# Gate/up pairs between the QKV blocks, h in two halves, and a last tile in halves, in a fused local-attention and GLU kernel

## The chip, the core and the metric

The kernel runs on one core of a Trainium2 chip. The metric is the device time of one execution in microseconds (us). A core has TensorE (PE, matmuls into PSUM), VectorE (DVE), ScalarE (ACT), GpSimd (POOL) and SyncE (SP). Each works through its own queue in order, and they wait for each other on semaphores. PEld is PE's loading of weights, which overlaps its matmuls. Transfers (DMA) are issued from the queues of SP, ACT and POOL.

## What is computed

The input x is 2048 rows of 512 values, bfloat16. Cut to what matters:

```
xn  = layernorm(x)                                  # per row
q, k, v = xn @ wqkv                                 # 32 heads of 16
logits[s, w] = q[s] . k[s - 2 w] / 4,  w = 0..7     # masked where s - 2 w < 0
o   = softmax(logits) @ v[s - 2 w];   s = o @ wo
y   = (gelu(xn @ w_gate) * (xn @ w_up)) @ w_down    # 512 -> 1792 -> 512
out = x + s * silu(y)
```

## The kernel before, in words

The rows are cut into four blocks of 512 (j = 0 to 3), each of four tiles of 128 rows. In a block:

- `layer_norm`: DVE takes the statistics of a tile (L303, L304), ACT a square root (L310) and DVE a reciprocal (L316) for blocks 0 and 1; for blocks 2 and 3 POOL does both (`rstd_pool`, L325, L328). DVE normalises (L335), PE transposes (L351), ACT or DVE copies the result into `xnT` (L359, L361).
- `qkv`: twelve groups of four matmuls of 512 columns (block 0: 96 matmuls of 256 columns, in two halves of rows), L430, each into a PSUM tile of the ring `psf` ("f", four tiles). ACT evacuates them: q (L443), k (L449), v (L454, `vst`, four buffers). v goes to DRAM (SP, L403) and comes back shifted for the eight window places as `v_arr` (POOL, four transfers per half block, L496, three buffers).
- `scores`: DVE multiplies q by four shifted k at once (L517, 128 x 2048) and adds pairs of products (L527). Per half of the window there are four products and two adds; PE sums what is left with 8 matmuls into L (L534), ACT takes exp (L546). PE sums over the window (L588), DVE inverts (L598), PE spreads the result (L606), ACT copies it (L616).
- `values`: DVE normalises (L626), multiplies by v (L639) and adds pairs (L649), PE sums into O (L656), ACT evacuates (L667).
- `ffn_pair`: for each of 14 column groups four matmuls for g and four for u (L710), ACT's gelu of g (L720), DVE's product with u, read from PSUM, into h (L727). h shares its buffer with `wqkv_sb`.
- `out_tile`: s from o and wo (L752), y from h and w_down (L764), silu (L775), gate (L778), residual (L785), store (L789). The last tile's s, gate, residual and store are cut at column 384; both parts of s lie in one PSUM tile.

The order of the instructions on each engine is fixed when the kernel is built. The class `Order` (L45) is a list scheduler. Every task has an engine, an assumed duration (the constants of L26 to L38), the tasks that it needs, a priority, and the buffers that it takes and frees; `run` always takes the task that can start first by these assumptions. HOP (L38) is the assumed delay from one engine to another. A chain of `add_main` tasks keeps the QKV, gate/up and output matmuls in program order on PE; transposes, L, sums and O are slotted in where the scheduler expects them to be ready. ACT also issues the loads of the weights (`load_weights`, L842 to L856). All HW transfers share eight semaphores in turn, so an issue can wait for the transfer eight places earlier.

Of the kernel before, what the change touches and what calls it, by code (L numbers as in the profile page):

```python
# [9 lines left out]
ALU = mybir.AluOpType  # L10
# [14 lines left out]

MM = 0.216  # L26
COL16 = 1.1
COL8 = 0.65
TR = 0.28
PROD = 1.14  # L30
HMUL = 0.6
STATS = 0.8
NORM = 0.36
TRCOPY = 0.36
ACT1 = 0.62
ACT2 = 1.06
TABLE = 1.28
HOP = 0.2  # L38
# [6 lines left out]
class Order:  # L45
# [45 lines left out]
    def run(self):  # L91
        left = list(self.tasks)
        while left:
# [10 lines left out]
            if t.eng == "dve" and t.prio >= 1.0:  # L104
                soon = [
                    (self.ready(u), u.seq, u) for u in left
                    if u.eng == "dve" and u.prio <= -1.5 and self.ready(u) is not None
                ]
                if soon and min(soon)[0] < s + 0.4:
                    s, _, t = min(soon)  # L110
# [20 lines left out]
def kernel(  # L131
# [23 lines left out]
    def pool(name, bufs, **kw):  # L155
# [8 lines left out]
    vapool = pool("vapool", 3)  # L164
    prpool = pool("prpool", 6)
# [6 lines left out]
    psf = pool("psf", 4, space=bass.MemoryType.PSUM)  # L172
    psa = pool("psa", 2, space=bass.MemoryType.PSUM)
# [5 lines left out]
        {"xn": 4, "q": 3, "vst": 4, "va": 3, "pr": 6, "attn": 2, "o": 2, "h": 1, "gl": 3, "sg": 3,  # L179
         "f": 4, "a": 2, "O": 1}  # L180
# [5 lines left out]
    wqkv_sb = hpool.tile([P, 3, NC * D + 64], BF16, name="wqkv_sb", tag="h")  # L186
    order.taken["h"].append("wqkv")
# [3 lines left out]
    wd_sb = wpool.tile([P, NF, D], BF16, name="wd_sb")  # L191
    wqkv_v = A_wqkv.rearrange("(k p) n -> p k n", p=P)

    for t in range(TPB):
        eng = nc.sync if t % 2 == 0 else nc.scalar
        eng.dma_start(out=x_sb[:, t, :], in_=x2d[t * P : (t + 1) * P, :])  # L196
# [12 lines left out]
    load_wqkv(0)  # L209
# [6 lines left out]
    x_there = [3.2, 3.5, 3.8, 4.1] + [9.5] * 2 + [12.0] * 2 + [13.5] * 4 + [16.0] * 4  # L216
# [12 lines left out]
    mhalf = cpool.tile([P, TPB], F32, name="mhalf")  # L229
    nc.gpsimd.memset(mhalf[:], -0.5)  # L230
# [63 lines left out]
    rstd_done = {}  # L294

    def layer_norm(j):
# [24 lines left out]
        def rstd_pool(t0, n, deps):  # L321

            def fn():
                r = rstd[:, t0 : t0 + n, 0]
                nc.gpsimd.tensor_scalar(  # L325
                    out=r, in0=mv[:, t0 : t0 + n, 1], scalar1=EPS, scalar2=None, op0=ALU.add
                )
                nc.gpsimd.tensor_tensor(out=r, in0=r, in1=mhalf[:, 0:n], op=ALU.pow)  # L328

            return add("pool", 1.4, fn, deps=deps, prio=prio)  # L330

# [14 lines left out]
        def transpose(t, dep, on_act):  # L346
            def fn():
                tiles["tr", t] = psa.tile([P, NC * P], BF16, name="tr_ps", tag="a")
                for c in range(NC):
                    cs = slice(c * P, (c + 1) * P)  # L350
                    nc.tensor.transpose(tiles["tr", t][:, cs], tiles["xn", t][:, cs], ident[:])  # L351
                if t < 2:
                    warm_up(2 + t, TQ // 2)
# [9 lines left out]
            a = add("pe", TR, fn, deps=[dep], prio=-1.0, takes=[("a", ("tr", t))], frees=[("xn", t)])  # L363
# [13 lines left out]
        elif j == 1:  # L377
            for half in range(2):
                pair = list(ts)[2 * half : 2 * half + 2]
                r = rstd_act(pair[0], 2, [stat(t) for t in pair])  # L380
                for t in pair:
                    transpose(t, norm(t, r), on_act=False)
        else:
            r = rstd_done[j] = rstd_pool(ts[0], TPB, [stat(t) for t in ts])
            for t in ts:
                transpose(t, norm(t, r), on_act=False)
# [10 lines left out]
    v_stored = {}  # L397

# [11 lines left out]
    def qkv(j):  # L410
# [4 lines left out]
        for lo in range(0, TQ, n):  # L415
            for which in range(3):
                for c in range(0, NC, w):
# [57 lines left out]
                    else:  # L475
                        st = add("sp", 0.6, store_v(j, c, lo, n, w), deps=[e], prio=-1.0)

                        v_stored[j] = add(
                            ("dma", key), 3.0, lambda: None, deps=[(st, 0.0)], frees=[("vst", key)]
# [5 lines left out]
    def load_values(j, half):  # L485
        def fn():
            v_arr = vapool.tile([P, DH // 2, VL], BF16, name="v_arr")
            tiles["va", j, half] = v_arr
            SP = PAD + S
            for w4 in range(4):  # L490
# [5 lines left out]
                nc.gpsimd.dma_start(out=v_arr[32 * w4 : 32 * (w4 + 1), :, :], in_=src)  # L496

        issue = add("pool", 2.4, fn, deps=[v_stored[j]], prio=-2.0, takes=[("va", (j, half))])
        v_ready[j, half] = add(("dma", "va", j, half), 7.5, lambda: None, deps=[(issue, 0.0)])
# [5 lines left out]
    def scores(j, prio):  # L505
        exps = []
        for w2 in range(2):
# [21 lines left out]
            def reduce(w2=w2, prods=prods):  # L529
                L = psa.tile([P, TQ], F32, name="L_ps", tag="a")  # L530
                tiles["L", j, w2] = L
                for i in range(2):
                    for w4 in range(4):
# [5 lines left out]
                            stop=(i == 1),  # L539
# [14 lines left out]
            for c in range(NC):  # L554
# [9 lines left out]
                if c % 2 == 1:  # L564
# [3 lines left out]
                            opens=key, closes=key if last else None, frees=[("pr", (*key, c))],  # L568
                        )
                    )  # L570
            r = add(
                "pe", COL8, reduce, deps=[ps[-1]], prio=-0.5, takes=[("a", ("L", j, w2))],
                frees=[("pr", (*key, c)) for c in (0, 2)],
# [44 lines left out]
        s = add("pe", 0.4, sums, deps=[(e, 0.3) for e in exps], prio=-0.4, takes=[("a", ("sum", j))])  # L618
        r = add("dve", 1.15, recip, deps=[s], prio=-1.5, frees=[("a", ("sum", j))])
        b = add("pe", 0.3, spread_back, deps=[r], prio=-0.4, takes=[("a", ("b", j))])  # L620
        b_ready[j] = add("act", ACT1, b_copy, deps=[b], prio=-0.6, frees=[("a", ("b", j))])

    def values(j, prio):
# [10 lines left out]
        for half in range(2):  # L634
# [39 lines left out]
            for i in range(4):  # L674
# [19 lines left out]
                "pe", COL8, reduce, deps=[ps[-1]], prio=-0.5, takes=[("O", (j, half))],  # L694
# [10 lines left out]
    def ffn_pair(j, fc):  # L705
# [17 lines left out]

        def mult():
            if fc == 0:
                tiles["h", j] = hpool.tile([P, NF, TQ], BF16, name="hT", tag="h")
            nc.vector.tensor_tensor(  # L727
                out=tiles["h", j][:, fc, :], in0=tiles["gl", j, fc][:], in1=tiles["u_ps", j, fc][:],
                op=ALU.mult,
            )  # L730
# [7 lines left out]
        h_ready[j, fc] = add(  # L738
            "dve", HMUL, mult, deps=[a, u], prio=-2.0, takes=[("h", j)] if fc == 0 else [],
            frees=[("f", ("u", j, fc)), ("gl", (j, fc))],  # L740
        )


    def out_tile(j, tt, split):
        t = j * TPB + tt
        last = tt == TPB - 1

        def s_mms(cs):
            if cs.start == 0:
                tiles["s", t] = psf.tile([P, D], F32, name="s_ps", tag="f")  # L750
            for c in range(NC):
                nc.tensor.matmul(  # L752
                    tiles["s", t][:, cs],
# [6 lines left out]
        def y_mms(lo, hi):  # L760
            if lo == 0:
                tiles["y", t] = psf.tile([P, D], F32, name="y_ps", tag="f")
            for fc in range(lo, hi):
                nc.tensor.matmul(  # L764
                    tiles["y", t][:],
                    lhsT=tiles["h", j][:, fc, tt * P : (tt + 1) * P],
                    rhs=wd_sb[:, fc, :],
# [4 lines left out]
        def silu():  # L772
            tiles["sil", t] = fpool.tile([P, D], BF16, name="sil")
            tiles["sg", t] = fpool.tile([P, D], BF16, name="sg")
            nc.scalar.activation(out=tiles["sil", t][:], in_=tiles["y", t][:], func=AF.Silu)  # L775

        def gate(cs):
            nc.vector.tensor_tensor(  # L778
                out=tiles["sg", t][:, cs], in0=tiles["sil", t][:, cs], in1=tiles["s", t][:, cs],
# [11 lines left out]
        edges = (0, D) if not split else (0, D - P, D)  # L791
        columns = [slice(a, b) for a, b in zip(edges, edges[1:])]
        y = None
        s = []

        def add_y():
            y = None
            for lo, hi in ((0, NF // 2), (NF // 2, NF)):
                y = add_main(
# [59 lines left out]
    for j in range(NJ):  # L859
        layer_norm(j)  # L860
# [46 lines left out]
```

The softmax here doesn't subtract the row's maximum and nothing guards it: scores larger than these inputs give would overflow.

## Time and profile before

| | us |
|---|---|
| median of 14 runs (lowest to highest) | 231.48 (230.47 to 232.1) |
| the profiled execution, and its span | 231.22, 229.5 |
| PE busy (share) | 222.0 (97%) |
| DVE busy (share) | 193.3 (84%) |
| ACT busy (share) | 111.1 (48%) |
| POOL busy (share) | 28.1 (12%) |
| TensorE clock granted, mean | 0.997 |
| one 128x512 matmul, from one start to the next | 0.216 |
| one product of 128x2048 on DVE, busy; from one start to the next | 1.22; 1.14 |

In the profile a row of a group reads: line, engine, operation, tiles (out<-in), shapes, count | busy time in all, mean ns of one | idle time just before, and what ended it. The chain of work that ended last is followed back from the last instruction: a piece is its start, its length and what it was; matmuls lie end to end there, while their rows overlap by about 0.16 us. The slices cut the span into 40 parts of 5.7 us; a digit is the busy share in tenths. A timeline line is start, length, engine, line and operation, with the idle time before it and what ended that in square brackets. ACTq and SPq are the queues that issue transfers.

### The profile page before, as it was taken

How to read it: one execution, taken by the hardware profiler on the slowest of the kernel's cores; microseconds unless marked ns; L12 is line 12 of the kernel's file. 1: busy time of each engine (PE TensorE's matmuls, PEld its weight loads, DVE VectorE, ACT ScalarE, POOL GpSimd, SP SyncE). 2: the span in 40 equal slices, each digit the busy share in tenths (PEclk: the TensorE clock that was granted, in tenths of full speed). 3: DMA queues.
4: the chain of work that ended last, by engine and by line, in shares of the span. 5: the costliest groups of instructions: out<-in, count | busy, mean ns of one | idle time of the engine just before them, and what ended most of it. 6: DMA issues, size and time to landing. Idle time of an engine off the chain costs nothing.

```text
span 229.5 us, 3272 instructions
## 1 busy us (share of the span) xinstructions
PE 222.0 (97%) x1234; PEld 105.0 (46%) x1234; DVE 193.3 (84%) x270; ACT 111.1 (48%) x167; POOL 28.1 (12%) x67
## 2 busy tenths in 40 slices
PE   7899999899999999999999999999999999999992
PEld 2897554354444434444444444444444444444441
DVE  4899999999999999999999999999759997343222
ACT  3566568477634365454435474434463164334211
POOL 7102930300412000040400002100000000000000
PEclk9999999999999999999999999999999999999998
DMA  5995799599828000054530010900000100000010
GB/s 153 350 381 175 158 205 362 167 281 339 206 38 186 3 0 23 23 123 111 119 68 3 0 46 23 211 0 0 1 3 23 46 23 1 3 0 0 23 45 25
DMA packets 15072, 22.64 MB, mean 99 GB/s; under 512 B 1472, under 2 KB 11984, under 8 KB 15056
## 3 DMA queue, kind: packets, MB, share of 16 engines
q0 software_dynamic: 2592, 8.54, 16.9%
q1 hardware_dynamic: 8592, 7.57, 10.5%
q10 hardware_dynamic: 3872, 6.32, 7.9%
q8 instruction: 9, 0.15, 0.3%
q14 instruction: 7, 0.06, 0.1%
HBM read 18.22 MB, written 4.21 MB: 98 GB/s over the span
## 4 chain that ended last, share of the span: by engine, by line
PE 94%; DMA 3%; DVE 1%; SPq 0%; ACT 0%; issue 0%; ACTq 0%; DVEq 0%
PE g_ps L710 21%; PE u_ps L710 21%; PE y_ps L764 21%; PE qkv_ps L430 18%; PE s_ps L752 6%; DMA wqkv_sb<-in_A_wqkv_dram 3%; PE L_ps L534 2%; PE O_ps L656 2%; PE tr_ps L351 1%; PE sum_ps L588 0%; PE b_ps L606 0%; SPq L196 0%; DVE sg L778 0%; ACT vst L454 0%; DVE sg L785 0%
## 5 line engine op out<-in xcount | busy, mean ns | idle before, releaser
L710 PE MATMUL g_ps<-xnT,wg_sb 128*128 128x512 bf16 x224 | 57.6, 379 | 0.0
L710 PE MATMUL u_ps<-xnT,wu_sb 128*128 128x512 bf16 x224 | 57.6, 379 | 0.0
L720 ACT ACTIVATE gl<-g_ps 128x512 bf16<-128x512 f32 x56 | 33.4, 597 | 48.8 <-PE g_ps L710 48.7
L764 PE MATMUL y_ps<-wd_sb,hT 128*128 128x512 bf16 x224 | 51.3, 379 | 0.0
L727 DVE TENSOR_TENSOR hT<-gl,u_ps 128x512 bf16<-128x512 bf16 x56 | 38.2, 685 | 12.5 <-PE u_ps L710 12.4
L430 PE MATMUL qkv_ps<-xnT,wqkv_sb 128*128 128x512 bf16 (+1 forms) x240 | 43.9, 337 | 1.4 <-ACT vst L454 0.8
L639 DVE TENSOR_TENSOR pv<-attn,v_arr 128x2048 bf16<-128x2048 bf16 x32 | 38.5, 1220 | 0.1
L517 DVE TENSOR_TENSOR prod<-q_sb,k_sb 128x2048 bf16<-128x2048 bf16 x32 | 38.4, 1222 | 0.0
L710 PEld LDWEIGHTS <-wg_sb 128*128 128x128 bf16 x224 | 21.4, 98 | 27.6 <-issue 2.5
L710 PEld LDWEIGHTS <-wu_sb 128*128 128x128 bf16 x224 | 21.6, 98 | 27.2 <-issue 1.7
L764 PEld LDWEIGHTS <-hT 128*128 128x128 bf16 x224 | 21.5, 98 | 25.7 <-issue 0.4
L430 PEld LDWEIGHTS <-wqkv_sb 128*128 128x128 bf16 x240 | 24.9, 108 | 16.8 <-issue 1.6
L496 POOL DMA_DIRECT2D v_arr<-vT_dram x32 | 18.6, 589 | 101.3 <-DVE pv L639 86.7
L775 ACT ACTIVATE sil<-y_ps 128x512 bf16<-128x512 f32 x16 | 9.6, 597 | 33.2 <-PE y_ps L764 33.1
L778 DVE TENSOR_TENSOR sg<-sil,s_ps 128x512 bf16<-128x512 bf16 (+2 forms) x17 | 11.1, 652 | 11.5 <-PE s_ps L752 7.7
L527 DVE TENSOR_TENSOR prod<-prod 128x2048 bf16<-128x2048 bf16 x16 | 19.6, 1223 | 0.2
L649 DVE TENSOR_TENSOR pv<-pv 128x2048 bf16<-128x2048 bf16 x16 | 19.5, 1222 | 0.2
L752 PE MATMUL s_ps<-wo_sb,o_sb 128*128 128x512 bf16 (+2 forms) x68 | 16.5, 367 | 0.0
L303 DVE BATCH_NORM_STATS2 stats<-x_sb 128x6 f32<-128x512 bf16 x16 | 10.8, 672 | 2.4 <-DMA x_sb<-in_A_x_dram 2.4
L454 ACT ACTIVATE vst<-qkv_ps 128x512 bf16<-128x512 f32 x16 | 9.4, 600 | 6.7 <-PE L_ps L534 3.4
L443 ACT ACTIVATE q_sb<-qkv_ps 128x512 bf16<-128x512 f32 x16 | 9.5, 604 | 4.8 <-PE qkv_ps L430 4.7
L449 ACT ACTIVATE k_sb<-qkv_ps 128x512 bf16<-128x512 f32 x16 | 9.2, 597 | 3.9 <-PE qkv_ps L430 3.9
(56 smaller groups left out, 120.7 us busy)
## 6 DMA issues: line engine op xcount, KB each, us to landing
v_arr<-vT_dram POOLq DMA_DIRECT2D x32, 260.0 KB, 5.4
vT_dram<-vst SPq DMA_DIRECT2D x16, 128.0 KB, 6.5
out_dram<-sg SPq DMA_DIRECT2D x15, 128.0 KB, 1.7
wg_sb<-in_B_w_gate_dram ACTq DMA_DIRECT2D x1, 1792.0 KB, 10.2
wu_sb<-in_B_w_up_dram ACTq DMA_DIRECT2D x1, 1792.0 KB, 15.3
wd_sb<-in_B_w_down_dram ACTq DMA_DIRECT2D x1, 1792.0 KB, 10.4
wqkv_sb<-in_A_wqkv_dram SPq DMA_DIRECT2D x3, 512.0 KB, 7.0
x_sb<-in_A_x_dram SPq DMA_DIRECT2D x2, 512.0 KB, 9.0
```

Of the source, the lines that this page charges most:

```text
L430: nc.tensor.matmul(ps[:, i * n : (i + 1) * n], lhsT=wqkv_sb[:, which, ws], rhs=xnT[:, dk, j * TQ + lo : j * TQ + lo + n], start=(dk == 0), ...
L496: nc.gpsimd.dma_start(out=v_arr[32 * w4 : 32 * (w4 + 1), :, :], in_=src)
L517: nc.vector.tensor_tensor(out=prod[:], in0=tiles["q", j][:, c, :].unsqueeze(1).to_broadcast([P, 4, TQ]), in1=kwin, op=ALU.mult,)
L527: nc.vector.tensor_tensor(out=a[:], in0=a[:], in1=b[:], op=ALU.add)
L639: nc.vector.tensor_tensor(out=pv[:], in0=tiles["attn", j][:, w2, :].unsqueeze(1).to_broadcast([P, 4, TQ]), in1=tiles["va", j, half][:, 4 * ...
L649: nc.vector.tensor_tensor(out=a[:], in0=a[:], in1=b[:], op=ALU.add)
L710: nc.tensor.matmul(ps[:], lhsT=w[:, dk, fc * P : (fc + 1) * P], rhs=xnT[:, dk, j * TQ : (j + 1) * TQ], start=(dk == 0), stop=(dk == NC - 1),)
L720: nc.scalar.activation(out=tiles["gl", j, fc][:], in_=tiles["g_ps", j, fc][:], func=AF.Gelu_apprx_tanh)
L727: nc.vector.tensor_tensor(out=tiles["h", j][:, fc, :], in0=tiles["gl", j, fc][:], in1=tiles["u_ps", j, fc][:], op=ALU.mult,)
L752: nc.tensor.matmul(tiles["s", t][:, cs], lhsT=tiles["o", j][:, c, tt * P : (tt + 1) * P], rhs=wo_sb[:, c, cs], start=(c == 0), stop=(c == ...
L764: nc.tensor.matmul(tiles["y", t][:], lhsT=tiles["h", j][:, fc, tt * P : (tt + 1) * P], rhs=wd_sb[:, fc, :], start=(fc == 0), stop=(fc == N ...
L778: nc.vector.tensor_tensor(out=tiles["sg", t][:, cs], in0=tiles["sil", t][:, cs], in1=tiles["s", t][:, cs], op=ALU.mult,)
```

## The change

- The scheduler's constants are new (`G`), and some priorities. The order of all engines follows from them.
- Seven gate/up pairs of block 0 are issued early: four after the QKV of block 1, three after that of block 2 (`BETWEEN`). h is two tiles, h0 (pairs 0 to 6) and h1 (pairs 7 to 13, in the buffer of `wqkv_sb`). wg and wu are loaded in two halves of columns each.
- For blocks 1 to 3 (`UPACT`) ACT copies u from PSUM into h, and DVE multiplies there in place.
- For blocks 2 and 3 (`FULL`) DVE adds the two remaining pair sums as well, and L takes 4 matmuls.
- `v_arr`: two transfers from POOL and two from SP; two buffers.
- Start: x tiles 0 and 1, then q's weights in two halves (SP and ACT), then x tiles 2 and 3, then the rest. The weights are laid out so that a partition holds four neighbouring rows, and the transposes take every fourth column. The two warm-up matmuls between the first two transposes are dropped.
- The reciprocal root of blocks 2 and 3 is done on ACT and DVE.
- The last tile is cut into two halves of 256 columns from y on, each half of y and s with its own PSUM tile.

The order that the changed program has: PE takes all 64 transposes before the last four matmuls of block 1's QKV; ACT has 19 table loads where there were 18.

```diff
+G = dict(
+    MM=0.217, COL8=0.3, COL4=0.2, TR=0.354, PROD=1.167, HMUL=0.582, HMUL2=0.34, STATS=0.881,
+    NORM=0.326, TRCOPY=0.444, ACT1=0.58, ACT2=1.087, TABLE=1.075, HOP=0.136, LOOK=0.275, vst=2.654,
+    vload=3.833, vissue=2.706, TRACT=(), x2=13.724, x3=17.04, FULL=(2, 3), UPACT=tuple((j, fc) for j in (1, 2, 3) for fc in range(14)),
+    BETWEEN={1: 4, 2: 3}, trig=[0, 0, 3, 3],
+    s_prio=[1.0, 2.0, 3.5, 4.0], v_prio=[1.5, 2.0, 3.75, 4.5], e_lat=0.1, b_lat=0.1, p_sum=-1.5,
+    p_red=-0.5, p_tr=-1.0, p_h=-1.4, wo_at=0, wd_at=1, fb=4, ab=2, ob=1, prb=6, vab=2, x_early=[3.2,
+    3.5, 3.8, 4.1],
+)
...
-HOP = 0.2
+HOP = G["HOP"]
...
+    load_tile(0, nc.sync)
+    load_tile(1, nc.scalar)
+    load_q(0, 2, nc.sync)
+    load_q(2, 4, nc.scalar)
+    load_tile(2, nc.sync)
+    load_tile(3, nc.sync)
     load_wqkv(1)
     load_x(4, 6)
     load_wqkv(2)
     load_x(6, 8)
     load_x(8, 12)
...
+                    nc.tensor.transpose(
+                        tiles["tr", t][:, c * P : (c + 1) * P], tiles["xn", t][:, c::NC], ident[:]
+                    )
...
+        a = add("pool", G["vissue"], lambda: fn(nc.gpsimd, (0, 1)), deps=[v_stored[j]], prio=-2.0, takes=[("va", (j, half))])
+        b = add("sp", 1.0, lambda: fn(nc.sync, (2, 3)), deps=[v_stored[j], (a, -G["vissue"])], prio=-2.0)
+        v_ready[j, half] = add(
+            ("dma", "va", j, half), G["vload"], lambda: None, deps=[(a, 0.0), (b, 0.0)]
+        )
...
+            def whole(prods=prods):
+                a, b = prods[0], prods[2]
+                nc.vector.tensor_tensor(out=a[:], in0=a[:], in1=b[:], op=ALU.add)
+
+            if full:
+                ps.append(
+                    add(
+                        "dve", PROD, whole, deps=[ps[-1]], prio=prio, opens=key, closes=key,
+                        frees=[("pr", (*key, 2))],
+                    )
+                )
...
-        s = add("pe", 0.4, sums, deps=[(e, 0.3) for e in exps], prio=-0.4, takes=[("a", ("sum", j))])
+        s = add("pe", 0.4, sums, deps=[(e, G["e_lat"]) for e in exps], prio=G["p_sum"], takes=[("a", ("sum", j))])
...
+        copied_up = (j, fc) in G["UPACT"]
+
+        def hidden():
+            n, i = divmod(fc, NF // 2)
+            if i == 0:
+                tiles["h", j, n] = hpool.tile([P, NF // 2, TQ], BF16, name="hT", tag=f"h{n}")
+            return tiles["h", j, n][:, i, :]
+
+        def evacuate():
+            nc.scalar.activation(out=hidden(), in_=tiles["u_ps", j, fc][:], func=AF.Copy)
+
         def mult():
-            if fc == 0:
-                tiles["h", j] = hpool.tile([P, NF, TQ], BF16, name="hT", tag="h")
-            nc.vector.tensor_tensor(
-                out=tiles["h", j][:, fc, :], in0=tiles["gl", j, fc][:], in1=tiles["u_ps", j, fc][:],
-                op=ALU.mult,
-            )
+            h = tiles["h", j, fc // (NF // 2)][:, fc % (NF // 2), :] if copied_up else hidden()
+            u = h if copied_up else tiles["u_ps", j, fc][:]
+            nc.vector.tensor_tensor(out=h, in0=tiles["gl", j, fc][:], in1=u, op=ALU.mult)
...
+        if copied_up:
+            v = add(
+                "act", ACT1, evacuate, deps=[u], prio=-0.5, takes=takes, frees=[("f", ("u", j, fc))]
+            )
+            h_ready[j, fc] = add(
+                "dve", G["HMUL2"], mult, deps=[a, v], prio=G["p_h"], frees=[("gl", (j, fc))]
+            )
...
+        columns = [slice(0, D)] if not split else [slice(0, D // 2), slice(D // 2, D)]
+
         def s_mms(cs):
-            if cs.start == 0:
-                tiles["s", t] = psf.tile([P, D], F32, name="s_ps", tag="f")
+            tiles["s", t, cs.start] = psf.tile([P, cs.stop - cs.start], F32, name="s_ps", tag="f")
...
+        for cs, ym, sm in zip(columns, y, s):
             end = cs.stop == D
+            a = add(
+                "act", ACT1, lambda cs=cs: silu(cs), deps=[ym], prio=-0.5, func="silu",
+                takes=[("sg", t)] if cs.start == 0 else [], frees=[("f", ("y", t, cs.start))],
+            )
...
+        half = DF // 2
+        when = [copied[2], q_ready[1], k_ready[1], q_ready[2], k_ready[2], q_ready[3], k_ready[0]]
+        for n, (w_sb, w) in enumerate(((wg_sb, B_w_gate), (wu_sb, B_w_up), (wg_sb, B_w_gate), (wu_sb, B_w_up))):
+            lo = n // 2 * half
+            start(
+                w_sb[:, :, lo : lo + half],
+                w.rearrange("(p k) n -> p k n", p=P)[:, :, lo : lo + half], when[G["trig"][n]],
+            )
...
+        if j in G["BETWEEN"]:
+            ffn_pairs(0, G["BETWEEN"][j])
```

## The prediction

> **What bounds the kernel now.** I read the slices first, then the chain of work that ended last, then the pieces of that chain and the timeline where it breaks.
>
> ```profile
> PE   7899999899999999999999999999999999999992
> DVE  4899999999999999999999999999759997343222
> ACT  3566568477634365454435474434463164334211
> PE 94%; DMA 3%; DVE 1%; SPq 0%; ACT 0%; issue 0%; ACTq 0%; DVEq 0%
> ```
>
> PE is full from the second slice to the last but one, and 94% of the chain is PE. DVE is just as full until slice 29, then has room; ACT has half of its time free. So only four things can shorten this kernel: less PE work, a gap inside PE's run, the time before it, the time after it. The pieces of the chain and the timeline show each:
>
> ```profile
> 1.71 6.01 DMA wqkv_sb<-in_A_wqkv_dram
> 7.76 2.81 PE qkv_ps L430 x24
> ...
> 43.03 0.57 PE L_ps L534 x8
> 43.72 0.61 ACT vst L454
> 44.37 1.89 PE qkv_ps L430 x8
> ...
> 80.73 0.55 PE L_ps L534 x8
> 81.28 0.97 PE u_ps L710 x4
> ```
>
> ```profile
> 40.32 3.28 ACTq L844 DMA_DIRECT2D wo_sb<-in_A_wo_dram  x3
> 43.72 1.08 ACT L454 ACTIVATE vst<-qkv_ps 128x512 bf16<-128x512 f32 x2 [3.39 <-PE L_ps L534]
> ...
> 224.09 1.04 PE L752 MATMUL s_ps<-wo_sb,o_sb 128*128 128x384 bf16 x8
> 225.22 0.55 DVE L778 TENSOR_TENSOR sg<-sil,s_ps 128x384 bf16<-128x384 bf16 x1 [2.75 <-PE s_ps L752]
> 225.81 0.36 DVE L785 TENSOR_TENSOR sg<-sg,x_sb 128x384 bf16<-128x384 bf16 x1
> 226.08 0.28 DVE L778 TENSOR_TENSOR sg<-sil,s_ps 128x128 bf16<-128x128 bf16 x1
> 226.40 0.23 DVE L785 TENSOR_TENSOR sg<-sg,x_sb 128x128 bf16<-128x128 bf16 x1
> ```
>
> PE starts its work at 7.76 and ends it at 225.14: 217.4 us. The one gap I find is 43.60 to 44.37, 0.77 us. ACT sits in the issues of wo: the fourth of them needs a DMA semaphore that wu holds, and wu (issued 27.70, 15.3 to landing) lands at 43.0. Four v evacuations stand behind it, and PE runs out of PSUM.
>
> **The change, part by part** (against the profiled execution: span 229.5, time 231.22, so 1.72 around the span).
>
> Gap at 43.6. In the new order wo's issues wait for older transfers (v loads of block 0, v stores of block 1), which by the old landing times (at most 11.5) are down by 44, and wo comes at about 47. ACT then only pays four issues at 0.61 = 2.4 us instead of the block from 40.3 to 43.6. Behind them stand one exp and four v evacuations; four PSUM tiles of 0.864 = 3.5 us cover that. Gain 0.77; it could be 0 if the cover fails. I take 0.77.
>
> L sums. For blocks 2 and 3 DVE adds the two pair sums once more (four adds) and each L needs 4 matmuls, not 8. A pass of four is half of 0.55 = 0.275; four L give 1.1. The lower bound is 4 x 0.216 (what 512 columns take in the g and u stream: 0.864 / 4) = 0.86. I take 1.0.
>
> Start. x tiles 0 and 1 and then q come first. q ceases to be the last wait: the copies into xnT end at 7.06 (ACT) and 7.32 (DVE), so PE could start 0.4 earlier. But the three weight loads take 6.0, 7.0 and 8.5 us to landing. q took 6.01; k must be the 7.0 (issued 2.18, lands 9.2, needed 9.64), so v lands at 3.27 + 8.5 = 11.8, and PE's v matmuls begin at 11.89. They have 0.1 us to spare. In the new order SP issues one transfer more ahead of k and v (about 0.3 later), and no byte less. So PE starts earlier and waits for v. I take 0, with bounds of -0.4 (v lands earlier too) and +0.3.
>
> Seven pairs between the QKV blocks. The same matmuls in another place of a full PE: 0. They start at 7.4 + block 0 (96 x 0.117 = 11.2) + 14 tiles of transposes at 0.225 (3.2) + block 1 (48 x 0.216 = 10.4) = 32.2 and need the first halves of wg and wu by then; these 1.8 MB are issued at the old place of wg, which took 10.2 from 10.84, so they land near 22. h in two halves lets pairs 0 to 6 write while wqkv_sb is still read. One deadline moves: all transposes now come before the end of block 1's QKV. The old DVE queue had its last norm at 32.2; the new one has two products and an add (3.4) less before it, two copies (0.7) and four reciprocals (0.6, rstd of blocks 2 and 3 comes from POOL to ACT and DVE) more: 30.1. Added up one by one (stats 0.80, norm 0.35, copy 0.35, product 1.14 apart, four sqrt of 0.29 on ACT hidden) I get 30.7. PE wants the last two tiles at 31.0. Cover 0.3 to 0.9.
>
> h product. For blocks 1 to 3 ACT copies u out of PSUM (42 x 0.597 = 25 us on ACT, which goes from 111 to 136) and DVE multiplies within SBUF. No row shows that product. Its nearest row is the residual, in place in SBUF: 0.425 against 0.685, and 0.345 against 0.60 from start to start. So DVE gains 42 x 0.255 = 10.7, loses 4 x 1.14 for the adds, and nothing of it is on the path. Per pair ACT has 1.2 us in PE's 1.73. The tight place is the start of blocks 1 and 2, with two table loads between the last silu and the first gelu. From the end of y: 0.2 + silu 0.60 + load 1.28 + exp 0.60 + load 1.28 + gelu 0.60 = 4.56; PE has L 0.44, s 0.86 and two pairs 3.46 = 4.76 before it needs that gelu's tile. Cover 0.2.
>
> ```profile
> L546 ACT ACT_TABLE_LOAD x6 | 7.7, 1283 | 0.1
> L785 DVE TENSOR_TENSOR sg<-sg,x_sb 128x512 bf16<-128x512 bf16 x15 | 6.4, 425 | 0.5
> L727 DVE TENSOR_TENSOR hT<-gl,u_ps 128x512 bf16<-128x512 bf16 x56 | 38.2, 685 | 12.5 <-PE u_ps L710 12.4
> ```
>
> Here the Trainium skill speaks against the change: "ScalarE: Activation LUTs", section "Table sets: the hidden batching unit", prices each switch to another set at about 2.7 us and asks to batch by set, and the change goes from 18 loads to 19 and puts more behind them. With 2.7 each of the two places would be 2 x 1.4 - 0.2 = 2.6 late, 5 us in all; with the row's 1.283 nothing. All loads of this trace are near that figure, so I take the row.
>
> v loads on two queues, two buffers for three. SP now waits for DVE to free a buffer. Behind it stand v stores of block 3 and output stores; for those wait only the evacuations and gates one ring of four or three later, tens of us on. v is there long before its product (the old loads waited 29 us for a buffer). 0; without that cover a load's 5.4 would show.
>
> Last tile. Each half has its own PSUM tile. PE: 28 matmuls of 256 columns at 2.81 / 24 = 0.117 (the QKV of block 0) for 14 of 0.216, and 8 for 8 in s: +0.15, between 0 and +0.3. DVE: today the first gate waits for all of s and DVE ends 1.49 after PE. Gate 256 is about 0.42, residual 0.29 (between the rows of 128 and 384). The first gate now runs during the second half of s, and after PE ends come residual, gate, residual: 1.1. Gain 0.4.
>
> New waits. Three covers of 0.2 to 0.3 above, and PE's order is fixed ahead with shorter hops than before (0.136 for 0.2; exp to sum 0.1 for 0.3), while a gelu here starts 0.2 after its matmuls' last slot. I take 0.5 in all, bounds 0 and 1.5.
>
> Sum: -0.77 - 1.0 + 0 + 0.15 - 0.4 + 0.5 = -1.5; 229.7 against 231.22. The median lies 0.26 above the profiled execution: 230.0.
>
> **The rivals.**
>
> - v's weights land earlier too and the covers hold: -0.4 and no 0.5 gives 229.1. For it: DMA is only half busy before 5.7 us. Against: it is full (1.05) from 5.7 to 11.5.
> - Small waits eat the gain: 24 sums on PE (L, sum, b, O) each 0.06 late is 1.5 instead of 0.5, and v late by 0.3: 231.3, no change. For it: PE is in order, every lateness of DVE is its own. Against: DVE has more room than before.
> - Slower: the product in SBUF stays at 0.60. From one L to the next in block 1, DVE then has 19 products or adds x 1.14 + 14 products h + 1.07 of gate and residual: 27.6 with 0.345, 31.2 with 0.60; PE has 28 x 0.864 + 1.3 + 0.86 + 1.5 = 27.9. PE waits 3.3 there and in block 2 (block 3 has no scores behind it): 230.0 + 6.6 = 236.6. It decides above 0.42 from start to start: (1.5 + 2 x 0.3) / 28 = 0.075 over 0.345. For it: no such row. Against: the residual's row has the same operands.
>
> **How the numbers follow.** Likeliest as summed, 0.60: 230.0. All holds, 0.13: 229.1. Small waits, 0.15: 231.3. Slow product, 0.12. A measurement tells about 0.2%, 0.46 us. Faster 0.73, same 0.15, slower 0.12. The range runs from just under the second case to just above the third, 228.9 to 231.7, and leaves out the last.
>
> **What would show it.** Right: no ACT wait before vst near 48; L of 4 matmuls at about 0.28; PE's v matmuls at 11.7 to 12.0 although q's began near 7.4; hT from SBUF near 0.42; DVE ending 1.1 after PE. Wrong: PE idle before a g (table loads), before tr_ps near 31 or before L, sum or O (DVE late); a product near 0.68.

## The result, and the profile after

The changed kernel takes 228.26 us (median of 10 runs, 228.23 to 228.45), the kernel before 231.48 (47 runs, 230.47 to 233.33): a ratio of 0.986, 95% interval 0.984 to 0.988. The forecast of 230.0 had the right sign and gave the gain less than half its size (1.5 for 3.2); 228.26 lies below the range. The profiled execution takes 228.24 with a span of 226.5; before it was 231.22 and 229.5. So 3.0 us have to be found in the trace.

First the slices (busy tenths of PE, DVE, ACT) and the shares of the chain of work that ended last, of the changed kernel:

```profile
PE   7999999999999999999999999999999999999993
DVE  4899999999999999899999999999936999322232
ACT  3566675658777346297777435877772187767210
PE 95%; DVE 2%; DMA 1%; issue 0%; DVEq 0%
```

The eighth slice, the only one in which PE's run was broken behind the start, is whole. DVE is about as full as before until slice 29, ACT works more, and the ACT entry has left the chain. No engine has become the bound in PE's place. The pieces of that chain at three places:

```profile
0.82 2.58 DMA x_sb<-in_A_x_dram
...
6.71 0.44 DVE xnT L366
7.29 2.78 PE qkv_ps L432 x24
10.07 0.45 PE tr_ps L354 x8
10.52 4.37 PE qkv_ps L432 x40
...
46.76 0.55 PE L_ps L546 x8
47.30 2.70 PE qkv_ps L432 x12
...
96.89 0.33 PE L_ps L546 x4
```

The reader is to see four things. The first transfer in the chain is the load of x where it was that of q's weights. PE begins its QKV at 7.29 where it was 7.76. At 10.52 it goes into forty QKV matmuls without a break, and v's are among them (the first of them at 11.23). An L of 4 matmuls takes 0.33 of the chain, an L of 8 still takes 0.55.

ACT's timeline around the issues of wo, and the timeline of the last tile:

```profile
45.94 2.60 ACTq L892 DMA_DIRECT2D wo_sb<-in_A_wo_dram  x4
48.58 0.60 ACT L558 ACTIVATE attn<-L_ps 128x512 bf16<-128x512 f32 x1 [2.05 <-PE qkv_ps L432]
49.08 2.06 ACT L456 ACTIVATE vst<-qkv_ps 128x512 bf16<-128x512 f32 x4
```

```profile
221.80 1.04 PE L796 MATMUL s_ps<-wo_sb,o_sb 128*128 128x256 bf16 x8
...
222.49 0.42 DVE L825 TENSOR_TENSOR sg<-sil,s_ps 128x256 bf16<-128x256 bf16 x1 [2.35 <-PE s_ps L796]
222.95 0.29 DVE L832 TENSOR_TENSOR sg<-sg,x_sb 128x256 bf16<-128x256 bf16 x1
223.16 0.42 DVE L825 TENSOR_TENSOR sg<-sil,s_ps 128x256 bf16<-128x256 bf16 x1
223.61 0.29 DVE L832 TENSOR_TENSOR sg<-sg,x_sb 128x256 bf16<-128x256 bf16 x1
```

Four issues of wo now take 2.60, and the chain goes on through PE at 47.30: the four v evacuations stand behind them without PE running out of PSUM. In the tail the first gate runs while PE still works at the second half of s. PE ends at 222.84 and DVE at 223.90, 1.06 later; before it was 1.50.

Two rows of groups belong to the h product and the table loads:

```profile
L763 DVE TENSOR_TENSOR hT<-gl,hT 128x512 bf16<-128x512 bf16 x42 | 17.6, 422 | 11.9 <-ACT hT L758 11.8
L558 ACT ACT_TABLE_LOAD x7 | 9.0, 1283 | 0.1
```

The 3.0 us term by term: PE's start 0.48; the gap at 43.6, 0.86; four L at 0.55 - 0.33, 0.87; DVE behind PE 0.43; from DVE's end to the end of the span 2.63 where it was 2.89, 0.26; the rest, 0.1, lies spread over the PE pieces. PE's losses are counted here from the start of one matmul to the start of the next: 0.77 of the gap is idle time, but the rows of neighbouring matmuls overlap, and the idle time leaves that out.

### The profile page after: what moved, and what is told of

Its sections match the earlier page's. It is cut to its first block, busy times and chain, and to the rows that moved or that the text cites. A ratio compares the mean times of both kernels' runs of the same rounds, so it can differ in the third digit from the quotient of the medians.

```text
span 226.5 us, 3294 instructions
## 1 busy us (share of the span) xinstructions
PE 220.7 (97%) x1230; PEld 106.1 (47%) x1230; DVE 188.0 (83%) x278; ACT 137.4 (61%) x215; POOL 14.8 (7%) x46
## 4 chain that ended last, share of the span: by engine, by line
PE 95%; DVE 2%; DMA 1%; issue 0%; DVEq 0%
PE y_ps L808 22%; PE g_ps L735 22%; PE u_ps L735 22%; PE qkv_ps L432 19%; PE s_ps L796 6%; PE O_ps L681 2%; PE tr_ps L354 2%; PE L_ps L546 2%; DMA x_sb<-in_A_x_dram 1%; DVE stats L318 1%; PE sum_ps L613 0%; DVE xn_t L339 0%; PE b_ps L631 0%; DVE sg L825 0%; DVE xnT L366 0%
## 5 line engine op out<-in xcount | busy, mean ns | idle before, releaser
L808 PE MATMUL y_ps<-wd_sb,hT 128*128 128x512 bf16 (+1 forms) x238 | 51.4, 367 | 0.0
L432 PE MATMUL qkv_ps<-xnT,wqkv_sb 128*128 128x512 bf16 (+1 forms) x240 | 43.6, 337 | 0.3 <-DVE xnT L366 0.3
L808 PEld LDWEIGHTS <-hT 128*128 128x128 bf16 x238 | 22.7, 98 | 24.6 <-issue 0.9
L820 ACT ACTIVATE sil<-y_ps 128x512 bf16<-128x512 f32 (+1 forms) x17 | 9.7, 572 | 34.8 <-PE y_ps L808 34.8
L758 ACT ACTIVATE hT<-u_ps 128x512 bf16<-128x512 f32 x42 | 25.1, 598 | 8.8 <-PE u_ps L735 8.5
L763 DVE TENSOR_TENSOR hT<-gl,hT 128x512 bf16<-128x512 bf16 x42 | 17.6, 422 | 11.9 <-ACT hT L758 11.8
L825 DVE TENSOR_TENSOR sg<-sil,s_ps 128x512 bf16<-128x512 bf16 (+1 forms) x17 | 11.1, 653 | 12.2 <-PE s_ps L796 8.2
L504 POOL DMA_DIRECT2D v_arr<-vT_dram x16 | 9.3, 586 | 138.8 <-DVE pv L664 122.8
L796 PE MATMUL s_ps<-wo_sb,o_sb 128*128 128x512 bf16 (+1 forms) x68 | 16.4, 367 | 0.0
```

The lines of the kernel that those rows point to most:

```text
L432: nc.tensor.matmul(ps[:, i * n : (i + 1) * n], lhsT=wqkv_sb[:, which, ws], rhs=xnT[:, dk, j * TQ + lo : j * TQ + lo + n], start=(dk == 0), ...
L758: nc.scalar.activation(out=hidden(), in_=tiles["u_ps", j, fc][:], func=AF.Copy)
L763: nc.vector.tensor_tensor(out=h, in0=tiles["gl", j, fc][:], in1=u, op=ALU.mult)
L796: nc.tensor.matmul(tiles["s", t, cs.start][:], lhsT=tiles["o", j][:, c, tt * P : (tt + 1) * P], rhs=wo_sb[:, c, cs], start=(c == 0), stop= ...
L808: nc.tensor.matmul(tiles["y", t, cs.start][:], lhsT=tiles["h", j, fc // (NF // 2)][:, fc % (NF // 2), tt * P : (tt + 1) * P], rhs=wd_sb[:, ...
```

## The experiments

My theory after the comparison: the gain is a sum of independent pieces at PE's start, at the gap, in L and in the tail, all on PE's path, and the seven early pairs and the copy of u on ACT only keep PE fed. Its rivals: the new order as a whole brings the gain (then undoing one piece would cost much more or much less than its term), and, for the start, chance in one profiled execution. Each group of variants ran on one chip beside the kernel before. The changed kernel was not run again there, so undone variants are set against its 228.26; its own runs lie within 0.22. One execution of each variant was profiled. Where a loss is named below, the pieces of that profile add up to its difference from the changed kernel's profile within 0.1, so that the loss is not one of the chip. Not undone by themselves are the split of `v_arr`, the reciprocal root and the constants of the scheduler; the terms above leave a rest of 0.1 for them.

### The start and the gap

**b_wo**: the kernel before, the fourth load of wo issued beside wd instead of behind the other three.

```diff
-        for e in range(4):
+        for e in range(3):
             start(wo_sb[32 * e : 32 * (e + 1), :, :], v[e], k_ready[2])
-        start(wd_sb[:], B_w_down.rearrange("(k p) n -> p k n", p=P), q_ready[3])
+        add("act", 0.5, lambda: None, deps=[k_ready[2]], prio=-3.0)
+
+        def last():
+            nc.scalar.dma_start(out=wo_sb[96:128, :, :], in_=v[3])
+            nc.scalar.dma_start(out=wd_sb[:], in_=B_w_down.rearrange("(k p) n -> p k n", p=P))
+
+        add("act", 0.5, last, deps=[q_ready[3]], prio=-3.0)
```

> The kernel before, with one edit: the fourth load of wo, whose issue waited for wu to land, is issued with wd's load later; the order of all other instructions is the same. Theory (the waiting issue is the gap of 0.77 us, and its length differs from run to run because it hangs on when wu lands): PE has no gap near 43.6, the span is near 228.7, the time is near 230.45 (231.22 - 0.77, which is also the lowest run of before, 230.47), and the runs lie within 0.5 us of each other, not within 2.9. Rival (the gap only moves, and the spread of before has another cause): 231.2 to 231.5, with runs as far apart as before.

Measured: 230.33 (229.92 to 230.82) against 231.17, ratio 0.996 (0.995 to 0.998). The wait at 43.6 is gone and 0.84 with it, as expected. The spread, expected below 0.5, is 0.9, where the kernel before had 1.4 beside it: this wait was not all that makes the runs differ. And PE's QKV began at 7.35 in this profile, with the old order of the first loads.

**b_start**: the kernel before with the new order of the first loads alone.

```diff
-        eng = nc.sync if t % 2 == 0 else nc.scalar
-        eng.dma_start(out=x_sb[:, t, :], in_=x2d[t * P : (t + 1) * P, :])
...
-    load_wqkv(0)
+    load_tile(0, nc.sync)
+    load_tile(1, nc.scalar)
+    load_q(0, 2, nc.sync)
+    load_q(2, 4, nc.scalar)
+    load_tile(2, nc.sync)
+    load_tile(3, nc.sync)
```

> The kernel before, with the new order of the first loads alone (x tiles 0 and 1, q in two halves on two queues, x tiles 2 and 3, then k and the rest); layout and all other instructions as before. Theory (the new order also moves more bytes early, so v lands before PE asks for it): PE starts near 7.3 and does not wait for v, the time falls by 0.45 to about 231.0. Rival (the recorded prediction: v lands no earlier, PE waits for it near 11.7): within 0.1 of 231.5.

Measured: 230.73 (230.06 to 231.32), ratio 0.998 (0.996 to 0.999): 0.44 less than 231.17. PE starts at 7.61, not near 7.3 (its first four transposes take 0.61, those of b_wo 0.40), and does not wait for v. The wait at 43.6 is there (0.6 before a vst, where it was 0.8), and so is a spread of 1.3. So the recorded step "PE starts earlier and waits for v" falls. The 0.44 is the number expected, but the start alone does not explain it: in this profile it is 0.15 earlier.

**a_start**: the changed kernel with the old order of the first loads.

```diff
-    load_q(0, 2, nc.sync)
-    load_q(2, 4, nc.scalar)
     load_tile(2, nc.sync)
-    load_tile(3, nc.sync)
+    load_tile(3, nc.scalar)
+    load_wqkv(0)
```

> The changed kernel with the old order of the first loads (x tiles 0 to 3, then q as one load on SP). PE and DVE have the same order. Theory: PE starts at 7.76 again and nothing later makes it up: 228.26 + 0.47 = 228.7. Rival (the start was given back later in the changed kernel too): 228.3.

Measured: 228.30 (228.29 to 228.32). The order is worth nothing here, and PE starts at 7.29 all the same: the rival's number, though not its reason, since nothing was lost that could be given back. Another part of the new start must do it too.

**b_pk**: the kernel before with only the new layout of wqkv, w_gate and w_up.

```diff
-    wqkv_v = A_wqkv.rearrange("(k p) n -> p k n", p=P)
+    wqkv_v = A_wqkv.rearrange("(p k) n -> p k n", p=P)
...
-        start(wu_sb[:], B_w_up.rearrange("(k p) n -> p k n", p=P), k_ready[1])
+        start(wu_sb[:], B_w_up.rearrange("(p k) n -> p k n", p=P), k_ready[1])
```

> The kernel before with only the new layout of the weight rows (a partition holds four neighbouring rows of wqkv, w_gate and w_up; the transposes take every fourth column). Theory A (layout decides q's landing): about 0.4 less, 230.6, PE's QKV starts at 7.3 to 7.5, and the spread shrinks by half; wg and wu, read in longer runs, land earlier too, and with wu the wait of 0.8 at 43.6 gets shorter, up to 0.8 more, 229.8. Theory B (layout does nothing): 231.0, spread of 1 us.

Measured: 229.98, ratio 0.996 (0.993 to 0.998), 1.18 less than 231.16, near theory A's lower figure. The profile shows both halves of it: q takes 5.54 to landing and PE starts at 7.35; wu takes 14.0 where it took 15.3, and the wait before vst is absent. Seven of twelve runs lie within 0.04 us (229.94 to 229.98), the others reach up to 232.42. The layout brings most runs to the floor, and does not keep all there.

**a_oldstart**: the changed kernel with the whole old start: the edit of a_start, and the layout and the two warm-up matmuls.

```diff
-    wqkv_v = A_wqkv.rearrange("(p k) n -> p k n", p=P)
+    wqkv_v = A_wqkv.rearrange("(k p) n -> p k n", p=P)
...
-                if t == 1:
-                    warm_up(3, TQ // 2)
+                if t < 2:
+                    warm_up(2 + t, TQ // 2)
```

> The changed kernel with the whole old start: old order of the first loads, weight rows laid out as before (a partition holds rows 128 apart, the transposes take neighbouring columns), and the two warm-up matmuls between the first two transposes. Theory A (the layout decides how long q's weights take, and so PE's start): 228.7 to 228.8, and a spread of runs of about 1 us as in the kernel before, against 0.03 with the old load order alone. Theory B (the start gained only by chance of the profiled execution, and the spread of before came from the issues of wo): 228.3, spread below 0.25. Theory C (the two warm-up matmuls hold the second transposes): 228.5, small spread, PE's QKV starting 7.4 to 7.6.

Measured: 228.28 to 229.18, median 228.48. Its profiled execution is the slowest of the six, and the chain says why:

```profile
1.73 6.38 DMA wqkv_sb<-in_A_wqkv_dram
8.15 2.81 PE qkv_ps L430 x24
```

Here q takes 6.38 and PE starts at 8.15, 0.86 later than in the changed kernel; the time is 0.92 longer. Four runs lie below 228.6. So I read the spread as q's landing, which with the old start sometimes is the last wait and sometimes not; the faster runs have no profile. Theory A has the mechanism and the spread, though its 228.7 to 228.8 lies above the median. C named the number of the median, but PE waits for q and not for the transposes.

**a_kp**: the changed kernel, the layout alone undone.

```diff
-    wqkv_v = A_wqkv.rearrange("(p k) n -> p k n", p=P)
+    wqkv_v = A_wqkv.rearrange("(k p) n -> p k n", p=P)
...
-                w.rearrange("(p k) n -> p k n", p=P)[:, :, lo : lo + half], when[G["trig"][n]],
+                w.rearrange("(k p) n -> p k n", p=P)[:, :, lo : lo + half], when[G["trig"][n]],
```

**b_newstart**: the kernel before with the whole new start, that is the edits of b_start and b_pk and this one:

```diff
-                if t < 2:
-                    warm_up(2 + t, TQ // 2)
+                if t == 1:
+                    warm_up(3, TQ // 2)
```

> The changed kernel with only the old layout of the weight rows (a partition holds rows 128 apart); the new order of the first loads stays. Theory (either of the two is enough: q loaded first, in halves from two queues, has time to spare with either layout, and only old order and old layout together make PE wait): 228.3, spread below 0.25, QKV from 7.3. Rival (the layout is what counts): 228.5 with a spread of 0.9, like the kernel with the whole old start.

> The kernel before with the whole new start: q first in halves, the new layout for all three weights, no warm-up between the first transposes. Theory (PE starts at 7.3 in every run, and wu, which lands 1.3 earlier by its layout, no longer holds the fourth wo issue until v's evacuations are due): 229.9, all runs within 0.3, so that of the 3.0 between the two kernels 1.2 to 1.3 are layout and order of loads, and 1.7 are L, last tile and the rest. Rival (the runs far above the median with the layout alone, up to 232.4, have another cause than q's landing): median 229.9, but a tail of runs above 231.

Measured: a_kp 228.34 (228.22 to 228.48); b_newstart 229.88 (229.78 to 230.02), ratio 0.993 (0.990 to 0.996), PE starting at 7.37. The times are those of the two theories. In these runs either the order or the layout is enough to take q off the critical path of the changed kernel (a_start has four runs, a_kp six); PE waited for q there only without both. But a_kp's profile starts at 7.48 and not at 7.3:

```profile
5.56 1.31 PE L354 MATMUL tr_ps<-ident,xn_t 128*128 128x128 bf16 x8 [0.27 <-DVE xn_t L339]
7.48 0.71 PE L432 MATMUL qkv_ps<-xnT,wqkv_sb 128*128 128x256 bf16 x5 [0.20 <-DVE xnT L366]
```

The eight transposes take 1.31, where a_start's take 1.09 and its QKV begins at 7.29. This execution is one of three at 228.43 to 228.48; the other three lie at 228.22 to 228.26. Three of the changed kernel's ten runs lie at 228.44 or 228.45 as well. So a step of 0.2 stays in the start with q off the path; what makes the transposes slower is not shown.

And the whole new start makes the kernel before 1.58 faster than its 231.46 and takes its spread from over 2 us to 0.24. It includes the gap, since wu lands earlier (14.2 after its issue).

**a_pad**: the transfer of zeros into v's padding issued from SP instead of POOL.

```diff
-    nc.gpsimd.dma_start(
+    nc.sync.dma_start(
         out=vT_dram[:, 0:PAD]
```

> The changed kernel with the small transfer of zeros into the padding of v's DRAM array issued from SP behind the loads of x, not from POOL. In the traces the second normalise on DVE ends at 6.2 to 6.3 whenever it starts (0.41 long from 5.88, 0.70 from 5.51), just behind the end of that issue on POOL (6.11 to 6.2). Theory (POOL's issue holds DVE): the normalise takes 0.41 again, PE's QKV starts 0.1 to 0.3 earlier than 7.29, 228.0 to 228.2. Rival (chance, or the time is given back where v's weights or the next transposes are due): 228.3.

Measured: 228.18 (228.03 to 228.29), inside the theory's interval and not to be told from 228.26. In its profile the normalise starts at 5.74 and takes 0.44, in the changed kernel's at 5.73 and 0.48: both start too late to tell. Whether POOL's issue holds DVE stays open.

### The L sums

**a_L8**: no block in FULL, as in the diff; **a_L4x4** has (0, 1, 2, 3) there, **a_L4x3** (1, 2, 3), **a_L4x023** (0, 2, 3). Only this constant changes; the scheduler then orders all engines anew.

```diff
-    FULL=(2, 3),
+    FULL=(),
```

> The changed kernel, but no block is in FULL: DVE doesn't add the two pair sums of blocks 2 and 3, and all L take 8 matmuls again. Theory (PE is the bound everywhere and each L of 4 saves what the traces show, 0.55 - 0.33 = 0.22): 4 x 0.22 = 0.9 longer, 229.1 to 229.2, and the L pieces of the chain show 0.55. Rival 1 (DVE was near its limit, and four adds of 1.14 less remove waits): 228.3 or less. Rival 2 (an L costs its full 0.275 to 0.3, with the hop): 229.4 or more.

Measured: 229.60 (229.45 to 229.73), 1.34 longer. All eight L pieces show 0.55, PE has no new wait, and it ends 0.86 later than in the changed kernel: what the theory said of L. The other 0.35 of this profile (229.45, the fastest of the five runs) lies behind PE:

```profile
223.71 0.42 DVE L825 TENSOR_TENSOR sg<-sil,s_ps 128x256 bf16<-128x256 bf16 x1 [2.70 <-PE s_ps L796]
```

The first gate of the last tile waits for both halves of s here, and DVE ends 1.41 after PE where it was 1.06. So rival 2's number came out, and not for its reason. Why the gate waits in this order is open.

> The changed kernel with FULL for all four blocks: four more adds of 1.14 on DVE (4.6 us), four more L of 4 matmuls. Theory (PE is the bound, DVE has room): 4 x 0.22 = 0.9 shorter, 227.4. Rival (DVE has no room in blocks 0 and 1, where it is full and must also do statistics, norms and copies): a wait takes the gain's place, 228.3 or more, with PE idle before L or before transposes.

> The changed kernel with FULL for blocks 1, 2 and 3. With four blocks PE lost 0.9 at L and won nothing, since it waited 0.8 for gelus behind table loads in block 2's and 3's part and DVE was late. Theory (two adds of 1.14 fit into block 1): 2 x 0.22 shorter, 227.8. Rival (the order shifts as with four blocks and a table load comes too late): 228.5 or more, with waits of PE before a g.

> The changed kernel with FULL for blocks 0, 2 and 3. With blocks 1, 2 and 3 PE waited 0.6 for a gelu of block 1 behind two table loads. Theory (it is the ACT order around block 1 that costs, and DVE has room for two adds in block 0): 227.8. Rival (DVE is full in block 0, and what it does later is late, or the order around the table loads shifts all the same): 228.3 or more.

Measured: 228.97 (228.96 to 229.05), 228.60 (228.57 to 228.78) and 228.82 (228.80 to 228.91). None is faster than 228.26, and none of the three theories that spoke of room holds. The chain of a_L4x023, in the stretch where block 1 begins its pairs:

```profile
96.05 0.60 ACT sil L820
96.66 1.28 ACT L745
97.95 0.60 ACT gl L745
98.57 1.28 ACT L558
99.86 0.60 ACT attn L558
100.46 0.49 ACT hT L758
100.97 1.28 ACT L745
102.26 0.61 ACT gl L745
```

The pieces of 1.28 are table loads, for gelu, exp and gelu behind a silu. They stand one behind the other with one function between, and PE waits at their end for a g tile. In the changed kernel the exp comes ahead of the first gelu there, with two loads. From start to start PE loses 0.58 here and 0.38 at a v evacuation at 49; its two shorter L give back 0.43. In a_L4x3 it loses 0.76 behind two loads (98.91 and 100.80), against 0.43; in a_L4x4 1.64 in four places, against 0.86. The differences, 0.53, 0.33 and 0.78, are the times measured within 0.1. So each shorter L is worth what the theory said, and the adds don't cost by DVE's time: L comes at another point, an exp falls between two gelus or an evacuation comes late, and ACT then is the chain. Leaving out block 0 or block 1 made no difference to this.

### Tail, pairs, copy

**a_tail**: the changed kernel, y of the last tile whole, s cut at 384 in one PSUM tile, as before.

```diff
-        columns = [slice(0, D)] if not split else [slice(0, D // 2), slice(D // 2, D)]
+        columns = [slice(0, D)] if not split else [slice(0, D - P), slice(D - P, D)]
...
-            tiles["s", t, cs.start] = psf.tile([P, cs.stop - cs.start], F32, name="s_ps", tag="f")
+            if cs.start == 0:
+                tiles["s", t] = psf.tile([P, D], F32, name="s_ps", tag="f")
...
-            for cs in columns:
+            for cs in [slice(0, D)]:
...
+        a = add(
+            "act", ACT1, lambda: silu(slice(0, D)), deps=[y[0]], prio=-0.5, func="silu",
+            takes=[("sg", t)], frees=[("f", ("y", t, 0))],
+        )
```

> The changed kernel with the old last tile (y whole, s cut at column 384 in one PSUM tile). Theory: DVE again ends 1.5 after PE instead of 1.04, and the end of the program behind it 0.27 later as in the profiles: 228.26 + 0.45 to 0.7 = 228.7 to 229.0. Rival (the halves cost PE what they save DVE, 0.15 to 0.3): 228.4.

Measured: 228.75 (228.56 to 228.77), 0.49 longer in the median and 0.33 from lowest to lowest. Its profile is one of the three runs at 228.75 to 228.77, and 0.2 of it is a QKV that starts at 7.49, behind eight transposes of 1.34 as in a_kp. So 0.33 is nearer to what the tail is worth. DVE ends 1.50 after PE, as before. From the issue of the last store to the end of the span it has 2.47, the changed kernel 2.57: the 0.26 of the comparison above has nothing to do with the halves.

**a_nopairs**: all 14 pairs of block 0 behind the last QKV.

```diff
-    BETWEEN={1: 4, 2: 3}, trig=[0, 0, 3, 3],
+    BETWEEN={}, trig=[0, 0, 3, 3],
```

> The changed kernel, but all 14 gate/up pairs of block 0 are back behind the QKV of block 3 (BETWEEN empty); table loads fall with it. Theory (the same matmuls in another place of a full PE, other engines hidden): 228.3, within 0.3. Rival (the pairs in between give DVE a head start that keeps PE fed, so that without them PE waits for q k products, L or transposes): 229.5 or more, with PE idle between 40 and 90. A third theory (the early pairs and their additional table loads cost): 227.8.

Measured: 228.68 (228.65 to 228.91), 0.4 longer; the theory allowed 0.3. From 34.9 to 42.6 the chain runs through ACT: evacuations of q and k, a table load of 1.28, and four issues of weights (0.5 to 0.64 each) among them, until PE waits 0.2 for a v evacuation (0.38 from start to start, so nearly all of the loss). That the early pairs help by spreading ACT's evacuations and issues out is how I read this; it is argued, not tested by itself. It is not DVE, as the rival had it.

**a_psum**: DVE multiplies u straight from PSUM in all blocks.

```diff
-    UPACT=tuple((j, fc) for j in (1, 2, 3) for fc in range(14)),
+    UPACT=(),
```

> The changed kernel, but DVE multiplies u straight from PSUM in all blocks as before (UPACT empty): ACT loses 42 copies of 0.598 (25 us), DVE gets 42 x 0.26 = 11 us more. Theory (DVE at 83% in mean, but full until slice 29; the product from PSUM takes 0.60 from start to start, and by the recorded count DVE then has 31.2 in a block where PE has 27.9): PE waits, 231 to 235, with waits before L in blocks 1 and 2. Rival (the planner moves enough DVE work to where DVE has room, as in the kernel before, which ran with this product): 228.3 to 229.3. If the latter, the copy on ACT is worth little by itself.

Measured: 228.99 (228.98 to 229.21), 0.7 longer: inside the rival's range and far from the theory's. The waits of PE:

```profile
PE g_ps L735 <- DVE hT L763: 0.5, 1, 0.5
```

One wait, near 147 in block 2, behind one product of values; from start to start it is 0.65, nearly all of the loss. The product takes 0.685 again, as counted, but PE meets DVE's lateness only once. So the copy to ACT is worth 0.7 here, not the 2 to 7 of the count. The scheduler knew of the slow product here (`HMUL`, 0.582) and could order for it; the recorded slower rival had one that the scheduler takes to be fast (`HMUL2`, 0.34), and that was not run.

## Why the prediction missed

**Gap at 43.6: right.** 0.77 of idle time as said (0.86 from start to start), four issues at 2.6 against 2.4 predicted. The experiments add that there were two ways to it: later wo, and an earlier wu.

**L sums: right in kind.** 0.22 for each L, at the lower bound (0.86) and not at 1.0; an L of 4 takes 0.33 and not half of 0.55. Undone, PE ends 0.86 later; the rest of the 1.34 is not L's.

**h product, v loads: right.** The product in SBUF takes 0.422 (nearest row 0.425), v_arr took 5.6 and 6.1 to landing and nobody on PE waits for it. The slower rival named the product at 0.60; with the product from PSUM forced back, the loss is 0.7, not 6.6. That the rival's count of one block leaves out what the order carries over from block to block is my reading, not tested.

**Table loads: the row was right, and the rule's direction too.** The prediction set the row of a load against the price of a whole switch. The Trainium skill's "ScalarE: Activation LUTs", section "What ACT_TABLE_LOAD costs", puts a switch together from a load of about 1283 ns, which all 19 loads here show, and a drain of about 1380 ns, which this trace does not show: where the next function is ready, 1.31 lie between the end of one and the start of the next. PE waits for no gelu. But the cover there is small, as I worked out (0.2): three orders that differ only in L's adds let PE idle 0.4 to 0.8 for gelus behind loads.

**Start: this step failed.** The prediction said that v would be the next wait ("PE starts earlier and waits for v. I take 0"); the term of 0 measured -0.48. I took k and v to land 7.0 and 8.5 after their issues, as in the trace of before. In the changed kernel k's load takes 5.2 and v's, issued at 4.07, takes 6.6:

```profile
L204 SPq DMA_DIRECT2D wqkv_sb<-in_A_wqkv_dram x1: 557/557/557, 4.1 to 4.1; - x1
DMA to landing us min/median/max: 6.6/6.6/6.6
```

v is down at 10.65, and its matmuls begin at 11.23 with nothing to wait for. The 8.5 was no price of that load: b_wo leaves the order and the layout of the first loads as they were, and v's takes 7.1 there. One profile's landing was carried over as if it were fixed. The case -0.4 stood as a bound and as a rival, "v's weights land earlier too and the covers hold", 229.1, at 0.13. It is the one that came true, and even it was too high, by the terms below that it does not change.

**New waits: this step failed.** I took 0.5 for three covers of 0.2 to 0.3 and for shorter hops; it measured 0. All covers held, and PE shows no wait of 0.2 or more behind 7.3. Of bounds 0 and 1.5 the lower was right. That they held is in part luck: the orders above with more adds, without the early pairs or without the copy each have such waits.

**Last tile: nearly right.** DVE behind PE: -0.43 against -0.4. PE's price of halves: +0.04 in y against +0.15. Undone it is about 0.33, where the sum had 0.25. The 0.26 behind DVE's end stood in no term, and what it hangs on is open.

**The median.** The forecast put it 0.26 above the profiled execution, and carried that distance over too. With the new start the median (228.26) lies on the profiled execution (228.24). I read the old distance as landings, q's and wu's, that move from run to run; only one execution of each kernel was profiled.

From 230.0 to 228.26: waits 0.5, start 0.48, behind DVE's end 0.26, median 0.24, the halves 0.14 (0.11 on PE, 0.03 on DVE), the gap 0.09, rest of PE 0.12, less 0.13 in L; together 1.7.

The same account from the experiments: the whole start with the gap is 1.58 in medians. What b_newstart leaves (229.88 to 228.26; 1.56 in the profiles) is L 0.87, DVE behind PE 0.43, the end behind DVE 0.12 and PE's start 0.09; it needs hardly any other cause. That the pieces add in every combination does not follow: without the early pairs 0.4 are lost and without the copy 0.7, which are in no term of this sum, since the kernel before has neither and shows no such wait. They belong to the order that the scheduler makes for each variant.

## What to carry to other kernels

Where a transfer is the last wait, its duration in one trace is one of several that can come, not a price: look at the spread of the runs first, and ask what happens if the load that you make the next wait lands a microsecond earlier. When each of two edits removes the same wait, undoing one shows nothing; undo both. And when PE is full, an add that DVE can afford may still cost if it moves an activation function across another one's table load on ACT. A variant's loss belongs to the piece undone only as far as its own trace shows it there: of 1.34 for L, 0.86 was L.

## What the runs showed of the hardware

The same 512 KB of q's weights, in the old order and the old layout, took 6.0, 4.9 and 6.4 us to landing in three profiles (before, b_wo, a_oldstart), and v's 8.5, 7.1 and 8.4. The versions in which PE can wait for a landing (q's, or wu's through the wo issue) spread by 0.9 to 2.9 us from run to run; the changed kernel, its variants but a_oldstart, and b_newstart repeat within 0.3.

With four neighbouring rows to a partition instead of rows 128 apart, wu as one load of 1792 KB landed after 14.0 and 14.2 us (b_pk, b_newstart), against 15.2 to 15.7 in three profiles. Loaded in halves of the columns, 896 KB each, it shows no such gain: 7.7 to 9.6 with the new layout, 8.2 to 8.5 with the old (a_kp, a_oldstart).

The clock granted was 0.995 to 1.0 in all the profiled executions. In a_kp and a_tail the runs that are 0.2 slower are those at 0.996 or 0.997, but b_newstart's runs at 0.997 are among its fastest, so that no rule comes out of it.

An ACT table load took 1.283 us for each function, and a switch 1.31 from the end of one function to the start of the next. A product of 128x512 in SBUF took 0.422 on DVE, against 0.682 with one operand in PSUM.
